# Where GpSimd's branch to the second path stands: behind the closing barrier, or in its own stream

## The chip, the cores and the metric

The kernel runs on one core of one Trainium2 chip. A core has five engines, each with an instruction stream of its own: TensorE (PE in the profile; its weight loads are shown apart as PEld), VectorE (DVE), ScalarE (ACT), GpSimd (POOL) and SyncE (SP). [...] The metric is the device time of one execution in microseconds (us), as the median of several runs. The profile's span is a shorter thing: it runs from the first to the last instruction of the program itself, and leaves out what the runtime does ahead of it and behind it.

## The reference: chunked attention, then a multiplicative feed-forward

```
# q, k, v: (8 batches, 8 heads, 576 rows, 64), in float32; chunks of 64 rows, so 9 a batch
scores = (1 / sqrt(64)) * q_chunk @ k_chunk.T     # 64 x 64, each chunk sees itself alone
scores = scores - max(scores, axis=-1)
attn   = exp(scores); attn = attn / (sum(attn, axis=-1) + 1e-9)
x      = (attn @ v_chunk), heads side by side     # 4608 tokens x 512
out    = ((x @ w1) * (x @ w2)) @ w3 @ w_out       # 512 -> 1024 -> 1024 -> 512, out 4608 x 512
```

## The kernel before

The program has two paths, and `tile_chunk_attention__then__multiplicative_ffn_kernel` (L536) joins them.

**The first path** (`fast_path`, L47) computes everything in bfloat16 on all engines. The 4608 tokens are cut into 18 steps of 256 (four chunks, `NP`), taken in pairs. Its work is written as short functions named by a letter, and the string `ORDER` (L9) lists by hand in which order they are called; every instruction keeps that order on its engine (`inorder`, L90). For step `p`: GpSimd issues the loads of q, k and v (L98), VectorE transposes q and k (`T`, L201), TensorE makes the scores (`S`), ScalarE takes their exponential (`E`, L234), TensorE multiplies by v, to which a column of ones is added so that the row sums come out beside the products (`P`). VectorE takes the reciprocal of the row sums into `rcs` (`N`, L261) and multiplies by it (L264). `X` and `H` put x into the layout that TensorE wants, `A` and `B` multiply by w1 and w2, `C` and `M` (L351, L366) form their product, `O` multiplies by `w3o`, which is w3 times w_out, made once on the chip (`V`, `W`, `Z`). `Y` (L396) copies the result out of PSUM and SyncE stores it (`Q`, L193). The last step, `O17` (L384 to L390), is copied and stored in three pieces.

**The check.** The first path takes no maximum off the scores, so it holds only while the row sums stay in a safe range. When the last reciprocals are there (L265), `do_check` (L270) counts in how many places `rcs` lies between 2^-60 and 2^60: two instructions on VectorE (L280, L281), then on GpSimd a sum over the partitions (L283), the number of places minus that sum as an integer, `bad` (L284), and a load of `bad` into a GpSimd register (L285). `ORDER` has nothing more for GpSimd after this. TensorE, VectorE, ScalarE and SyncE still have the last steps of the feed-forward ahead of them, down to `O17`.

**The closing.** L538 and L539 close the first path before the second one is written. The profile puts the closing's instructions under L539: SyncE waits for every semaphore of the first path, the last output stores among them; all engines meet at a barrier; GpSimd clears the semaphores; all engines meet again.

**The second path** (`second_path`, L452) does the whole computation again, slowly and with the maximum taken off, in float32 on GpSimd alone, and overwrites `out`. It stands under `with g.If(bad != 0)` (L501): GpSimd compares the register and, when `bad` is zero, jumps over the body. The body is long. The search for the row maximum alone (L516, L517) is written out 63 times, each with its wait and its clearing of the semaphore (`done`, L480), and no other engine has an instruction in it. With the inputs of this case `bad` is zero: the trace has no instruction of the body, and the branch at L501 is the last instruction of the span.

Of the kernel before, what the change touches and what calls it, by code (L numbers as in the profile page):

```python
# [43 lines left out]


@with_exitstack
def fast_path(  # L47
    ctx: ExitStack,
    tc: tile.TileContext,
    q: bass.AP,  # L50
# [8 lines left out]
    nc = tc.nc  # L59
    B, H, S, D = q.shape  # L60
# [3 lines left out]
    CH = 64  # L64
    NCH = S // CH
    NT = B * S
    DM = H * D
    DF = moe_w1.shape[1]
# [11 lines left out]
    f32 = mybir.dt.float32  # L80
# [23 lines left out]
    w1 = wpool.tile([P, KO, DF], bf, name="w1")  # L104
    w2 = wpool.tile([P, KO, DF], bf, name="w2")

    w3 = wpool.tile([P, DF // BL, DF // NB], bf, name="w3")
# [341 lines left out]
    return flag[0]  # L449


def second_path(tc, bad, q, k, v, w1, w2, w3, w_out, out):  # L452


    nc = tc.nc
    B, H, S, D = q.shape
    CH = 64
    NCH = S // CH
    DM, DF = w1.shape
    KB = 4  # L460
    f32 = mybir.dt.float32
    op = mybir.AluOpType
    g = nc.gpsimd
    with ExitStack() as ctx:
        def sb(name, *shape):
            return ctx.enter_context(nc.sbuf_tensor(name, [CH, *shape], f32))

        loaded = ctx.enter_context(nc.semaphore("loaded"))
        worked = ctx.enter_context(nc.semaphore("worked"))
        qt, kv, prod, s = sb("qt2", D), sb("kv2", CH, D), sb("prod2", CH, D), sb("s2", CH)  # L470
        m, e, euler, minus1 = sb("m2", 1), sb("e2", CH), sb("euler", CH), sb("minus1", 1)
        x, wb, a, b, o = sb("x2", DM), sb("wb2", KB, DF), sb("a2", DF), sb("b2", DF), sb("o2", DM)

        def move(dst, src):
            g.dma_start(dst, src).then_inc(loaded, 16)
            g.wait_ge(loaded, 16)
            g.dma_reset(range(loaded.num, loaded.num + 1))
            g.sem_clear(loaded)

        def done(ins):  # L480
            ins.then_inc(worked, 1)
            g.wait_ge(worked, 1)
            g.sem_clear(worked)

        def fold(t, n):
            while n > 1:
                n //= 2
                done(g.tensor_tensor(t(0, n), t(0, n), t(n, 2 * n), op.add))

        def times(dst, src, w, n, width):  # L490

            done(g.memset(dst[:], 0.0))
            p = prod[:].rearrange("c a b -> c (a b)")[:, 0:KB * width].rearrange("c (i n) -> c i n", i=KB)
            wt = wb[:, :, 0:width]
            with g.Fori(0, n // KB) as i:
                move(wt, w[bass.ds(i * KB, KB), :].partition_broadcast(CH))
                done(g.tensor_tensor(p, wt, src[:, bass.ds(i * KB, KB)].to_broadcast([CH, KB, width]), op.mult))
                fold(lambda lo, hi: p[:, lo:hi], KB)
                done(g.tensor_tensor(dst[:], dst[:], p[:, 0], op.add))

        with g.If(bad != 0):  # L501
            done(g.memset(euler[:], math.e))
            done(g.memset(minus1[:], -1.0))
            with g.Fori(0, B) as bi, g.Fori(0, NCH) as ci:
                with g.Fori(0, H) as hi:
                    def rows(t):
                        return t[bass.ds(bi, 1), bass.ds(hi, 1), bass.ds(ci * CH, CH), :]

                    move(qt[:], rows(q).rearrange("b h p d -> p (b h d)"))
                    move(kv[:], rows(k).rearrange("b h p d -> (b h p) d").partition_broadcast(CH))  # L510
                    done(g.tensor_tensor(prod[:], kv[:], qt[:].unsqueeze(1).to_broadcast([CH, CH, D]), op.mult))
                    fold(lambda lo, up: prod[:, :, lo:up], D)
                    done(g.tensor_scalar(s[:], prod[:, :, 0], 1.0 / math.sqrt(D), None, op.mult))
                    move(kv[:], rows(v).rearrange("b h p d -> (b h p) d").partition_broadcast(CH))
                    done(g.tensor_copy(m[:], s[:, 0:1]))
                    for j in range(1, CH):  # L516
                        done(g.tensor_scalar(m[:], m[:], s[:, j:j + 1], None, op.max))  # L517
                    done(g.tensor_scalar(s[:], s[:], m[:], -100.0, op.subtract, op.max))
                    done(g.tensor_tensor(e[:], euler[:], s[:], op.pow))
                    done(g.tensor_copy(s[:], e[:]))  # L520
                    fold(lambda lo, up: s[:, lo:up], CH)
                    done(g.tensor_scalar(m[:], s[:, 0:1], 1e-9, None, op.add))
                    done(g.tensor_tensor(m[:], m[:], minus1[:], op.pow))
                    done(g.tensor_scalar(e[:], e[:], m[:], None, op.mult))
                    done(g.tensor_tensor(prod[:], kv[:], e[:].unsqueeze(2).to_broadcast([CH, CH, D]), op.mult))
                    fold(lambda lo, up: prod[:, lo:up, :], CH)
                    done(g.tensor_copy(x[:, bass.ds(hi * D, D)], prod[:, 0, :]))
                times(a, x, w1, DM, DF)
                times(b, x, w2, DM, DF)
                done(g.tensor_tensor(b[:], a[:], b[:], op.mult))  # L530
                times(a, b, w3, DF, DF)
                times(o, a, w_out, DF, DM)
                move(out[bass.ds((bi * NCH + ci) * CH, CH), :], o[:])


def kernel(tc, *args):  # L536
    bad = fast_path(tc, *args)
    tc.close()  # L538
    tc.compile()  # L539
    second_path(tc, bad, *args)  # L540


# [28 lines left out]
```

## Time and profile before

| what | us |
|---|---|
| median of 3 runs | 247.47 (247.06 to 248.05) |
| the profiled execution's own time | 247.53 |
| its span, first to last instruction of the program | 243.1 |
| time of that execution outside its span | 4.43 |
| TensorE busy with matmuls | 225.4 (93% of the span) |
| VectorE, ScalarE, GpSimd busy | 154.4, 85.1, 83.7 |
| SyncE's last store issued (start) | 240.4 |

A line of the page or of an answer reads: line of the kernel, engine, operation, tile written <- tiles read, count, then durations. A `q` behind an engine's name means its sequencer: such instructions (waits, branches, register loads, barriers) are not counted as busy, and the timeline doesn't list them; the view of one source line does. There the three figures with slashes are the least, the middle and the greatest duration in ns, and the two behind them are the starts of the first and the last of them in us from the span's start.

### The profile page before, as it was taken

How to read it: one execution, taken by the hardware profiler on the slowest of the kernel's cores; microseconds unless marked ns; L12 is line 12 of the kernel's file. 1: busy time of each engine (PE TensorE's matmuls, PEld its weight loads, DVE VectorE, ACT ScalarE, POOL GpSimd, SP SyncE). 2: the span in 40 equal slices, each digit the busy share in tenths (PEclk: the TensorE clock that was granted, in tenths of full speed). 3: DMA queues.
4: the chain of work that ended last, by engine and by line, in shares of the span. 5: the costliest groups of instructions: out<-in, count | busy, mean ns of one | idle time of the engine just before them, and what ended most of it. 6: DMA issues, size and time to landing. Idle time of an engine off the chain costs nothing.

```text
span 243.1 us, 6361 instructions
## 1 busy us (share of the span) xinstructions
PE 225.4 (93%) x2731; PEld 120.0 (49%) x2753; DVE 154.4 (63%) x235; ACT 85.1 (35%) x116; POOL 83.7 (34%) x114
## 2 busy tenths in 40 slices
PE   1289999999999989999999999999999999999994
PEld 1147877874455444444444444444444444444443
DVE  1755899689799588999998899918540332143000
ACT  2411423423243343525336334162332332322322
POOL 7856874665995345574260230000000000000000
PEclk9999999999999999999999999999999999999999
DMA  6999999999999999999999893735502200400244
GB/s 174 179 185 181 185 169 199 197 191 172 166 171 219 213 234 241 176 219 200 207 222 241 230 150 84 168 88 206 143 0 89 86 0 0 175 1 1 86 173 173
DMA packets 93595, 37.63 MB, mean 155 GB/s; under 512 B 75008, under 2 KB 86528, under 8 KB 93568
## 3 DMA queue, kind: packets, MB, share of 16 engines
q0 software_dynamic: 82592, 18.88, 84.5%
q1 hardware_dynamic: 9936, 17.83, 24.5%
q10 hardware_dynamic: 1040, 0.52, 0.8%
q8 instruction: 21, 0.34, 0.6%
q14 instruction: 6, 0.05, 0.1%
HBM read 38.80 MB, written 9.44 MB: 198 GB/s over the span
## 4 chain that ended last, share of the span: by engine, by line
PE 89%; DMA 3%; DVE 3%; issue 2%; ACT 1%; SPq 1%; DVEq 0%
PE ab_ps L95 49%; PE o_ps L95 26%; PE w_ps L95 6%; PE pv L95 3%; PE s_ps L95 3%; PE z_ps L95 3%; DMA raw<-in_q_dram 2%; DVE qkT L201 1%; DMA qkm<-qkT 1%; SPq L193 1%; DVE xt L297 1%; DVE xn L264 1%; ACT qk L144 0%; ACT e L234 0%; DVE ab L366 0%
## 5 line engine op out<-in xcount | busy, mean ns | idle before, releaser
L95 PE MATMUL ab_ps<-xt,w 128*128 128x512 bf16 (+1 forms) x681 | 127.0, 342 | 0.9 <-DVE xt L297 0.3
L95 PEld LDWEIGHTS <-w 128*128 128x128 bf16 x704 | 67.1, 98 | 56.0 <-issue 1.8
L366 DVE TENSOR_TENSOR ab<-a_sb,ab_ps 128x512 bf16<-128x512 f32 x71 | 47.8, 674 | 43.6 <-ACT a_sb L351 43.4
L351 ACT COPY a_sb<-ab_ps 128x512 f32<-128x512 f32 x71 | 41.6, 586 | 80.8 <-PE ab_ps L95 80.6
L95 PE MATMUL o_ps<-w3o,ab 128*128 128x512 bf16 (+1 forms) x285 | 63.3, 373 | 0.6
L201 DVE STREAM_TRANSPOSE qkT<-qk 128x1024 bf16<-128x1024 bf16 x36 | 45.0, 1289 | 6.8 <-ACT qk L144 5.4
L95 PEld LDWEIGHTS <-ab 128*128 128x128 bf16 x296 | 28.5, 98 | 32.3
L98 POOL DMA_DIRECT2D vbuf<-in_v_dram x40 | 34.0, 856 | 19.8 <-PE ab_ps L95 4.9
L396 ACT COPY o_sb<-o_ps 128x1024 f32<-128x1024 f32 x17 | 17.2, 1013 | 45.3 <-PE o_ps L95 41.3
L264 DVE TENSOR_TENSOR xn<-pv,rcs 128x512 bf16<-128x512 f32 x36 | 24.9, 692 | 1.4
L98 POOL DMA_DIRECT2D qk<-in_q_dram x23 | 18.1, 791 | 9.8 <-DMA vbuf<-in_v_dram 2.5
L98 POOL DMA_DIRECT2D qk<-in_k_dram x23 | 18.0, 782 | 6.8 <-DMA vbuf<-in_v_dram 4.5
L234 ACT ACTIVATE e<-s_ps 128x1024 bf16<-128x1024 f32 x16 | 15.9, 1028 | 2.2 <-PE s_ps L95 2.0
L95 PE MATMUL w_ps<-wo,w3T 128*128 128x512 bf16 x62 | 13.9, 379 | 0.1
L305 DVE STREAM_TRANSPOSE xm<-xn 128x512 bf16<-128x512 bf16 x20 | 13.5, 696 | 0.2
L261 DVE RECIPROCAL rcs<-pv 128x8 f32<-128x8 f32 x36 | 7.0, 193 | 10.4 <-PE pv L95 10.4
L98 POOL DMA_DIRECT2D w<-in_moe_w_dram x16 | 11.1, 695 | 5.4 <-DMA vbuf<-in_v_dram 1.8
L95 PEld LDWEIGHTS <-e 64*32 64x32 bf16 (+1 forms) x832 | 7.8, 97 | 8.6 <-issue 6.8
L95 PE MATMUL pv<-vbuf,e 64*32 64x65 bf16 (+1 forms) x832 | 10.2, 198 | 1.6 <-ACT e L234 1.1
L297 DVE STREAM_TRANSPOSE xt<-xn 128x512 bf16<-128x512 bf16 x16 | 11.4, 711 | 0.5
L95 PEld LDWEIGHTS <-qkT 32*64 32x64 bf16 x512 | 5.6, 117 | 10.6 <-DVE qkT L201 7.9
L389 DVE COPY o_sb<-o_ps 128x256 f32<-128x256 f32 x1 | 0.4, 425 | 16.0 <-PE o_ps L95 16.0
(29 smaller groups left out, 53.7 us busy)
## 6 DMA issues: line engine op xcount, KB each, us to landing
out_dram<-o_sb SPq DMA_DIRECT2D x17, 512.0 KB, 2.9
qkm<-qkT SPq DMA_DIRECT2D x40, 128.0 KB, 4.4
vbuf<-in_v_dram POOLq DMA_DIRECT2D x32, 128.0 KB, 8.1
w<-in_moe_w_dram POOLq DMA_DIRECT2D x16, 256.0 KB, 9.6
qk<-in_q_dram POOLq DMA_DIRECT2D x11, 256.0 KB, 7.4
qk<-in_k_dram POOLq DMA_DIRECT2D x11, 256.0 KB, 7.8
xt<-xm SPq DMA_DIRECT2D x40, 64.0 KB, 3.1
wo<-in_moe_w_out_dram POOLq DMA_DIRECT2D x4, 256.0 KB, 7.9
```

Source lines behind the costliest of these rows:

```text
L95: return inorder(nc.tensor.matmul(*a, **kw))
L98: return inorder(nc.gpsimd.dma_start(dst, src))
L193: inorder(nc.sync.dma_start(dst, src))
L201: inorder(nc.vector.transpose(qkT_t[g][:, :, p % 2, s, heads(h)].rearrange("p e h (y t) -> p h t e y", t=2), qk_t[p][:, s, heads(h)].rearr ...
L234: inorder(nc.scalar.activation(e_t[p][:, :, heads(hh)], s_t[p][:].rearrange("p u (h q) -> p u h q", q=CH)[:, :, heads(hh)], Exp, scale=sca ...
L261: inorder(nc.vector.reciprocal(rc, pv[:, :, :, D:W]))
L264: inorder(nc.vector.tensor_mul(xn_t[p][:, u], pv[:, :, :, 0:D], rc.to_broadcast([P, 2, 4, D])))
L297: inorder(nc.vector.transpose(new_xt(g)[:].rearrange("p (o t) -> p o t", o=KO)[:, :, t0:t0 + UT] .rearrange("p o (m y) -> p m o y", y=BL), ...
L305: inorder(nc.vector.transpose(xm_t[g][:, u, :, m].rearrange("p o (c y) -> p c o y", y=BL), xn_t[p][:].rearrange("p u r m d -> p (u r) m d" ...
L351: inorder(nc.scalar.copy(a_t[p, j][:], ps_t[p, j][:, 0, :]))
L366: inorder(nc.vector.tensor_mul(o, view(a_t.pop((p, j))[:]), view(ps_t.pop((p, j))[:, 1, :])))
L396: inorder(nc.scalar.copy(o_sb[:], ps_t.pop(p)[:]))
```

## The change

The branch and the body of the second path move into the same tile program as the first path. `second_path` is called while that program is still open; `g.If` becomes `tc.If`, and the body becomes a critical section that GpSimd itself guards (`sync_engine` Pool, without a drain of GpSimd). The body's buffers come from a tile pool in place of raw tensors, and its two semaphores from the program's own allocator. The two lines that closed the first path ahead of the second one are gone: the program closes once, when the caller's `with` ends (L566 of before). The operations of the body are the same, one level less indented. `fast_path` is renamed `first_path` and is otherwise as it was.

```diff
-def fast_path(
+def first_path(
...
-def second_path(tc, bad, q, k, v, w1, w2, w3, w_out, out):
+@with_exitstack
+def second_path(ctx, tc, bad, q, k, v, w1, w2, w3, w_out, out):
...
-    with ExitStack() as ctx:
+    pool = ctx.enter_context(tc.tile_pool(name="second", bufs=1))
+    with tc.If(bad != 0), tc.tile_critical(sync_engine=mybir.EngineType.Pool, no_gpsimd_drain=True):
         def sb(name, *shape):
-            return ctx.enter_context(nc.sbuf_tensor(name, [CH, *shape], f32))
-
-        loaded = ctx.enter_context(nc.semaphore("loaded"))
-        worked = ctx.enter_context(nc.semaphore("worked"))
+            return pool.tile([CH, *shape], f32, name=name)
+
+        loaded, worked = tc.alloc_semaphore("loaded"), tc.alloc_semaphore("worked")
...
-        with g.If(bad != 0):
-            done(g.memset(euler[:], math.e))
-            done(g.memset(minus1[:], -1.0))
...
+        done(g.memset(euler[:], math.e))
+        done(g.memset(minus1[:], -1.0))
...
 def tile_chunk_attention__then__multiplicative_ffn_kernel(tc, *args):
-    bad = fast_path(tc, *args)
-    tc.close()
-    tc.compile()
-    second_path(tc, bad, *args)
+    second_path(tc, first_path(tc, *args), *args)
```

More of the change, by code (lines that the diff above doesn't have):

```diff
@@ L499, in times @@
                 done(g.tensor_tensor(dst[:], dst[:], p[:, 0], op.add))
-        with g.If(bad != 0):
-            done(g.memset(euler[:], math.e))
-            done(g.memset(minus1[:], -1.0))
[L504 to L533, printed above, removed]
@@ new lines, in second_path, with rows @@
+        done(g.memset(euler[:], math.e))
+        done(g.memset(minus1[:], -1.0))
+        with g.Fori(0, B) as bi, g.Fori(0, NCH) as ci:
+            with g.Fori(0, H) as hi:
+                def rows(t):
+                    return t[bass.ds(bi, 1), bass.ds(hi, 1), bass.ds(ci * CH, CH), :]
+                move(qt[:], rows(q).rearrange("b h p d -> p (b h d)"))
+                move(kv[:], rows(k).rearrange("b h p d -> (b h p) d").partition_broadcast(CH))
+                done(g.tensor_tensor(prod[:], kv[:], qt[:].unsqueeze(1).to_broadcast([CH, CH, D]), op.mult))
+                fold(lambda lo, up: prod[:, :, lo:up], D)
+                done(g.tensor_scalar(s[:], prod[:, :, 0], 1.0 / math.sqrt(D), None, op.mult))
+                move(kv[:], rows(v).rearrange("b h p d -> (b h p) d").partition_broadcast(CH))
+                done(g.tensor_copy(m[:], s[:, 0:1]))
+                for j in range(1, CH):
+                    done(g.tensor_scalar(m[:], m[:], s[:, j:j + 1], None, op.max))
+                done(g.tensor_scalar(s[:], s[:], m[:], -100.0, op.subtract, op.max))
+                done(g.tensor_tensor(e[:], euler[:], s[:], op.pow))
+                done(g.tensor_copy(s[:], e[:]))
+                fold(lambda lo, up: s[:, lo:up], CH)
+                done(g.tensor_scalar(m[:], s[:, 0:1], 1e-9, None, op.add))
+                done(g.tensor_tensor(m[:], m[:], minus1[:], op.pow))
+                done(g.tensor_scalar(e[:], e[:], m[:], None, op.mult))
+                done(g.tensor_tensor(prod[:], kv[:], e[:].unsqueeze(2).to_broadcast([CH, CH, D]), op.mult))
+                fold(lambda lo, up: prod[:, lo:up, :], CH)
+                done(g.tensor_copy(x[:, bass.ds(hi * D, D)], prod[:, 0, :]))
+            times(a, x, w1, DM, DF)
+            times(b, x, w2, DM, DF)
+            done(g.tensor_tensor(b[:], a[:], b[:], op.mult))
+            times(a, b, w3, DF, DF)
+            times(o, a, w_out, DF, DM)
+            move(out[bass.ds((bi * NCH + ci) * CH, CH), :], o[:])
```

## The prediction

> **What bounds the kernel now.** I read the page first, for the engine that fills the span.
>
> ```profile
> span 243.1 us, 6361 instructions
> ...
> PE 225.4 (93%) x2731; PEld 120.0 (49%) x2753; DVE 154.4 (63%) x235; ACT 85.1 (35%) x116; POOL 83.7 (34%) x114
> ...
> POOL 7856874665995345574260230000000000000000
> ...
> PE 89%; DMA 3%; DVE 3%; issue 2%; ACT 1%; SPq 1%; DVEq 0%
> ```
>
> TensorE makes 89% of the chain that ended last. GpSimd's row of slices (6.08 us each) goes empty in its last third. Nothing that GpSimd does there is on the chain within the span. So a change to GpSimd alone can win only at the very end, where all engines must meet, and I looked there next: GpSimd's timeline from 135 us on, then the source lines that the change touches.
>
> ```profile
> 140.28 1.79 POOL L98 DMA_DIRECT2D vbuf<-in_v_dram  x2
> 169.47 0.35 POOL L283 CROSS_LANE_REDUCE all_good<-good 128x1 f32<-128x1 f32 x1 [27.41 <-DVE both L281]
> 169.92 0.18 POOL L284 TENSOR_SCALAR bad<-all_good 1x1 int32<-1x1 f32 x1
> ```
>
> ```profile
> L285 POOLq TENSOR_LOAD <-bad x1: 746/746/746, 170.1 to 170.1; - x1
> ```
>
> ```profile
> L539 SPq EVENT_SEMAPHORE  x12: 17/28/28, 240.7 to 243.0; - x12
> L539 POOLq EVENT_SEMAPHORE  x4: 17/17/17, 242.3 to 243.0; - x4
> L539 POOLq DRAIN  x3: 46/92/971, 171.0 to 242.8; - x3
> ```
>
> ```profile
> L501 POOLq COMPARE_BRANCH  x1: 50/50/50, 243.1 to 243.1; - x1
> ```
>
> `bad` is in GpSimd's register at 170.1 + 0.75 = 170.9 us. GpSimd then begins the closing's drain (171.0) and does nothing until the closing barrier (242.3 to 243.0). Only behind that barrier comes the branch, as the last instruction of the span. Its 50 ns look like nothing. But 247.53 - 243.1 = 4.43 us of this execution lie outside the span, and the branch stands at their head. The DMA view of the stretch 243.1 to 248 us (40 slices of 0.12 us) shows what happened in them:
>
> ```profile
> GB/s 0 0 0 0 0 0 0 0 0 0 67 0 0 0 0 0 0 0 0 0 0 0 0 0 0 0 0 67 0 0 0 0 0 0 0 0 0 0 0 0
> DMA packets 2, 0.02 MB, mean 3 GB/s; under 512 B 0, under 2 KB 0, under 8 KB 0
> ## 3 DMA queue, kind: packets, MB, share of 16 engines
> q14 instruction: 2, 0.02, 1.0%
> ```
>
> Two packets of instructions, and nothing else. By the trace's own records they are 8192 bytes each; the first starts at 244.334 and takes 0.307. The trace also keeps every update of every semaphore, past the last instruction too. Semaphore 2, which no instruction of the program uses, counts the engines in before the runtime resets the others: 243.333, 243.367, then nothing until 246.464, then 246.507, 246.530 and on. In the next round of the same semaphore the steps are 247.538, .572, .610, .654, .677, so 34, 38, 44 and 23 ns. **The third arrival is late.** It should come 38 ns after the second, at 243.405, and comes 3.059 us later; the fourth follows it by the usual 43 ns, so nobody else was late by then. All other engines left the closing barrier at the same 243.05; only GpSimd had something between, the branch. I read this as GpSimd jumping to a place whose instructions weren't in its buffer, fetching them (the packet begins 1.2 us after the branch), and the whole core waiting for it.
>
> **The change part by part.**
>
> *The branch moved to the register load.* Its cost where it stands now: 246.464 - 243.405 = 3.06 us, all on the path that sets the end. Where it will stand: about 170.9 us, plus 0.05 for itself, plus the same 3.06, so GpSimd is through by some 174.1 us (177.5 if a second fetch is paid as well). Its next appointment is the closing barrier at 242.3 us: 65 us of cover or more, TensorE's matmuls of steps 14 to 17 being what hides it. If the cover were gone, the price would be the 3.06 again. It issues no DMAs of data; its instruction fetch, 8 KB a packet, meets SyncE's last transposing moves (L193, the last at 174.4) for some 0.3 us on one queue, and none of those is near the chain. GpSimd's own queue is empty by then: its last load is at 140.28.
>
> *What the 3.06 us leave late next.* Without the branch, GpSimd leaves its last barrier instruction at 243.0 + 0.02, ahead of the others (243.04 to 243.05), and the first engine reached semaphore 2 at 243.333, 0.3 us after that. If GpSimd needs no longer, it is third at 243.405 as the chain wants. No row shows GpSimd's own way from there without a miss, so I bound it. At best it is on time and the gain is 3.06. At worst all that lies between the packet's landing (244.641) and its arrival (246.464), 1.82 us, is its own work rather than the fetch; then it arrives at 243.01 + 1.82 = 244.84 and the gain is 246.46 - 244.84 = 1.62. I take 3.06, because in the next round of that barrier GpSimd's place in the chain costs 38 ns, no more than the others', and because this is the nearest row.
>
> *The closing itself* stays one closing: the same waits of SyncE, two barriers and a clear. The section may add a semaphore or two to SyncE's waits. They go by at about 61 ns each (240.73 to 242.25), and only those behind the last store's landing (242.06) count: 0 to 0.12 us. It may as easily reorder them in our favour by as much. I take 0.
>
> *Buffers and semaphores.* The body's pool lies over memory that the first path has used, and the body writes `out`, so the section must wait for nearly everything. Inside the jumped-over body these waits cost nothing. Ahead of the branch they would cost the gain (first rival below).
>
> Sum: 247.53 - 3.06 + 0 = 244.47 against the profiled execution; that stands 0.06 above the median of the runs, so I forecast **244.4**, 1.2% less. Its own range is 243.9 to 245.0, from the 1 us that the runs before spread over.
>
> [...] The row has 50 ns for the instruction but 3.06 us until the engine is seen again. [...]
>
> **The rivals.**
>
> *Part of the gap is GpSimd's own* (above): 247.47 - 1.62 = 245.9. For it: 1.8 us pass after the packet has landed, and I don't see what fills them. Against: the 38 ns.
>
> *The change doesn't do what it says:* the waits for memory and `out` are put ahead of the branch. Then GpSimd branches when the last store has landed, 242.06 + 0.05, is back after 3.06 at 245.2, the closing barrier (242.34 to 243.08, 0.74 us) follows to 245.9, and 0.33 later the chain's third arrival is at 246.25, against 246.46 before. That is 247.47 - 0.2 = 247.3, no change. For it: the section does depend on all of that. Against: the section stands inside the If, and its waits with it.
>
> *Slower:* the region is fenced, all engines meeting before the branch and again behind it, since a region that is scheduled as one piece may be closed off so. The If comes last in the program, so both fences stand at the end, at the price of the closing's own row, 0.74 us each, with the branch and its fetch still between: 247.47 + 1.47 = 248.9 (a single fence gives 248.2, within 0.5%). It decides as soon as an engine other than GpSimd has an instruction of the If. Against: only GpSimd holds the register and works in the body.
>
> **How the numbers follow.** Chances: forecast 0.70, part of the gap 0.13, waits ahead of the branch 0.12 (a single fence is counted here), two fences 0.05. 0.5% is 1.24 us, about what a measurement of this kernel can tell from no change. Faster by more is the first two, 0.83; same is 0.12; slower 0.05. The range takes in the first two with their spread: 243.9 to 246.1.
>
> **What would show it.** Right: the span still near 242.8 to 243.1, now ending with the closing's semaphores and not with a branch; the COMPARE_BRANCH at 171 to 172 us; an instruction packet about 1.2 us behind it; no packet right behind the span's end; semaphore 2 counting through without a gap, and time outside the span down from 4.43 to about 1.4 us. The second rival would show the branch still at 242 us; the third, barrier rows of the If on several engines; the first, a gap of some 1.5 us left before the third arrival with no branch in front. The prediction is wrong above all if GpSimd, having jumped early, must fetch again at the end: its closing and the runtime's part lie right behind the target and should come in sequence, but no row shows that.

## The result, and the profile after

The changed kernel takes 244.23 us (median of 4 runs, 243.97 to 245.27) against 247.50 (247.06 to 248.05, now four runs, the profiled one counted): a ratio of 0.9875 with a 95% interval of 0.9839 to 0.9911. The profiled execution took 244.48 us, with a span of 242.9.

The lines of the page that answer to those of before:

```profile
span 242.9 us, 6385 instructions
...
PE 226.7 (93%) x2753; PEld 120.2 (49%) x2753; DVE 154.3 (64%) x235; ACT 85.2 (35%) x116; POOL 83.7 (34%) x114
...
POOL 7856976656986345764160230000000000000000
...
PE 72%; DMA 16%; DVE 4%; SPq 3%; POOL 2%; issue 1%; ACT 0%; DVEq 0%; POOLq 0%
```

Within the span nothing has moved: the engines' busy times and GpSimd's empty last third are those of before. (TensorE's 226.7 us against 225.4 go with 22 more matmul records; a second execution of the changed kernel, e10 below, has 225.6 with the count of before.) TensorE's share of the chain fell from 89% to 72%, but that isn't the change: between loads and transposes that end nearly together the chain is followed back by one or the other, and a second execution of the same changed kernel shows 70%.

The branch and the closing, by source line:

```profile
L466 POOLq EVENT_SEMAPHORE  x2: 17/17/17, 173.6 to 173.7; - x2
L466 POOLq COMPARE_BRANCH  x1: 45/45/45, 170.8 to 170.8; - x1
```

```profile
L563 SPq EVENT_SEMAPHORE  x12: 17/28/28, 240.6 to 242.9; - x12
L563 POOLq EVENT_SEMAPHORE  x4: 17/17/17, 242.2 to 242.8; - x4
L563 POOLq DRAIN  x3: 46/98/971, 173.8 to 242.7; - x3
```

The branch itself still takes 45 ns, and GpSimd's next instruction starts 2.75 us after it (170.828 to 173.579). The two fetches that used to stand behind the span have come along. The first (171.81 to 172.42) lies between the branch and that next instruction; the second starts at 174.20, when GpSimd has already gone on. The DMA view of 170.8 to 175 us has both among SyncE's moves:

```profile
q1 hardware_dynamic: 324, 0.43, 40.8%
q14 instruction: 2, 0.02, 1.6%
```

and the same view of 242.9 to 248 us is empty:

```profile
GB/s 0 0 0 0 0 0 0 0 0 0 0 0 0 0 0 0 0 0 0 0 0 0 0 0 0 0 0 0 0 0 0 0 0 0 0 0 0 0 0 0
DMA packets 0, 0.00 MB, mean 0 GB/s; under 512 B 0, under 2 KB 0, under 8 KB 0
```

Semaphore 2 now counts 243.162, 243.197, 243.411, 243.455, 243.478, and its last update is at 244.843 instead of 247.895. From GpSimd's last closing semaphore (242.995 before, 242.824 after) to that last update it is **4.90 us before and 2.02 after: 2.88 us less**. The other 0.17 of the 3.05 by which the two profiled executions differ is an earlier arrival at the closing: TensorE's last matmul ends at 239.64 in place of 239.81. Spans of one kernel scatter by more than that (242.4 to 243.7 over the four runs of after), so I don't put it down to the change.

### The profile page after: what moved, and what is told of

It reads as the page before. It is cut to its first block, busy times and chain, and to the rows that moved or that the text cites. A ratio compares the mean times of both kernels' runs of the same rounds, so it can differ in the third digit from the quotient of the medians.

```text
span 242.9 us, 6385 instructions
## 1 busy us (share of the span) xinstructions
PE 226.7 (93%) x2753; PEld 120.2 (49%) x2753; DVE 154.3 (64%) x235; ACT 85.2 (35%) x116; POOL 83.7 (34%) x114
## 4 chain that ended last, share of the span: by engine, by line
PE 72%; DMA 16%; DVE 4%; SPq 3%; POOL 2%; issue 1%; ACT 0%; DVEq 0%; POOLq 0%
PE ab_ps L95 39%; PE o_ps L95 23%; PE w_ps L95 6%; DMA w<-in_moe_w_dram 4%; DMA qkm<-qkT 3%; SPq L193 3%; DMA qk<-in_q_dram 3%; DMA qk<-in_k_dram 3%; DMA xt<-xm 3%; PE pv L95 2%; PE s_ps L95 2%; DVE qkT L201 2%; POOL vbuf L98 1%; POOL w L98 1%; DVE xt L297 1%
```

## The experiments

My theory: a jump whose target is far ahead in GpSimd's stream makes it fetch instructions, and whoever waits for GpSimd waits for that. The first rival: it is the place that costs, a second piece of program behind the closing, whatever the jump's length. The second: the early section gains or costs something by its form. Medians scatter by some 0.5 us here, so beside them I use the **tail**, a number that doesn't depend on the matmuls: from the start of GpSimd's last closing semaphore to the runtime's last update of semaphore 2, by the trace's records.

| kernel | median us | ratio to before (95% interval) | tail us | third arrival after the second, us |
|---|---|---|---|---|
| before | 247.50 | | 4.90 | 3.097 |
| after | 244.23 | 0.9875 (0.9839 to 0.9911) | 2.02 | 0.214 |
| e1 short body, late branch | 245.12 | 0.9918 (0.9901 to 0.9934) | 2.35 | 0.392 |
| e2 short body, early branch | 245.10 | 0.9907 (0.9889 to 0.9924) | 2.02 | 0.214 |
| e3 no second path | 244.78 | 0.9895 (0.9878 to 0.9911) | 2.01 | 0.202 |
| e4 two late branches | 250.47 | 1.0138 (1.0121 to 1.0155) | 7.77 | 5.934 |
| e5 jump over some 214 | 247.42 | 1.0001 (0.9985 to 1.0017) | 4.81 | 2.975 |
| e6 jump over some 118 | 245.08 | 0.9917 (0.9894 to 0.9939) | 2.83 | 0.751 |
| e7 early branch, late count | 248.44 | 1.0062 (1.0038 to 1.0086) | 2.02 | 0.214 |
| e8 as e2, padded | 244.52 | 0.9884 (0.9865 to 0.9904) | 2.01 | 0.202 |
| e9 as e1, padded | 245.26 | 0.9915 (0.9894 to 0.9936) | 2.20 | 0.392 |
| e10 after, again | 244.70 | 0.9882 (0.9860 to 0.9905) | 2.04 | 0.214 |
| e11 no second path, again | 244.29 | 0.9884 (0.9856 to 0.9911) | 2.03 | 0.201 |

e5 was run eight times, e6 twice, after and the other experiments four times each. Each ratio is to runs of before on the same chip: 247.22 for e1 to e4, 247.08 for e5 to e7, 247.44 for e8 to e11.

**e1: the late branch with a short body.**

```diff
         with g.If(bad != 0):
             done(g.memset(euler[:], math.e))
             done(g.memset(minus1[:], -1.0))
-            with g.Fori(0, B) as bi, g.Fori(0, NCH) as ci:
-                with g.Fori(0, H) as hi:
...
-                move(out[bass.ds((bi * NCH + ci) * CH, CH), :], o[:])
```

> The kernel before, with the branch still behind the closing barrier, but the body of the second path cut to its first two fills (its loops are left out; they don't run on these inputs), so that the jump lands a few instructions on. Theory (the price is the fetch of a far target): no instruction packet behind the span, semaphore 2 counts through, and the time falls by what the change saved, to 244.3 (244.0 to 244.7), with the branch still the span's last instruction. Rival (the price is that a branch, or a second piece of program, stands behind the closing at all): 247.5 as before.

The branch is still the last instruction of the span, and nothing is fetched behind it (source line, then DMA view of 242.9 to 248 us):

```profile
L501 POOLq COMPARE_BRANCH  x1: 50/50/50, 242.9 to 242.9; - x1
```

```profile
DMA packets 0, 0.00 MB, mean 0 GB/s; under 512 B 0, under 2 KB 0, under 8 KB 0
```

The time falls by 2.10 us and the tail by 2.55. The rival, "the place costs", would have left 247.5 and is out: the length of the jump is what costs. I had expected 244.0 to 244.7 and got 245.12; 0.33 of the tail stays, which e9 takes apart.

**e2: the early branch with the same short body.** The same loops are left out of the changed kernel.

> The changed kernel with the same cut body (loops left out). Theory: GpSimd goes on within 0.2 us of the branch at 170.8, not 2.75 us; the time doesn't move, 244.2 (243.9 to 244.6), since 65 us covered the fetch. Rival (the early branch still cost something at the end, by its section's semaphores and boundary): below 243.7.

GpSimd goes on 0.19 us after the branch, and the tail is the changed kernel's to a hundredth:

```profile
L466 POOLq EVENT_SEMAPHORE  x2: 17/17/17, 171.5 to 171.6; - x2
L466 POOLq COMPARE_BRANCH  x1: 45/45/45, 171.3 to 171.3; - x1
```

So the 2.75 us that follow the branch in after, at 171 us, are covered wholly (tail 2.02 in both). The median of 245.10 is above what I expected. Part of it is in the closing of the profiled execution, which lies ahead of the tail: 1.01 us between GpSimd's two releases of the barrier, where after has 0.57 (see e8).

**e3 and e11: no second path.** The two closing lines and the call of `second_path` are taken out of before.

```diff
     bad = fast_path(tc, *args)
-    tc.close()
-    tc.compile()
-    second_path(tc, bad, *args)
```

> The kernel before without any second path (the whole of it left out), the count and the load of bad kept. Theory: 244.2 (243.9 to 244.6), as after: nothing of the branch is left on the path. In the changed kernel the third arrival at semaphore 2 comes 0.214 us after the second instead of 0.038; if that is GpSimd's own work behind the last barrier it shows here too, if it belongs to the section it is gone and the time is 0.18 lower. Rival (the section costs time elsewhere): 243.5 or less.

> The kernel without any second path once more, beside the changed one. Theory (the changed kernel has nothing of the branch left on its path): the same time within 0.4 us. Rival (the early section costs something yet): faster than the changed kernel by 0.5 us or more.

The tail is 2.01 and 2.03 us. The third arrival comes 0.20 us after the second here too, without any branch: that is GpSimd's own. In both traces L285 has only a wait of 17 ns, so the load of `bad`, which was to be kept, is out as well; it stood in GpSimd's idle stretch.

> The changed kernel, unaltered, on the chip of the runs beside it, to be set against the one without a second path. 2.01 us from GpSimd's last closing semaphore to the runtime's last count, a time of 244.3 (243.9 to 244.9).

The changed kernel took 244.70 us here, with a tail of 2.04. The medians miss two of the expectations narrowly: e3's 244.78 is above 244.6, and e11's 244.29 is 0.41 below e10, where 0.4 was named. The single runs of each spread over 0.7 to 1.1 us, and the ratios, 0.9882 and 0.9884, are alike. Nothing of the branch is left that these runs could tell, and no run points to a version that beats the changed kernel.

**e4: two far jumps in a row.** `second_path` is called twice behind the closing, with buffers and semaphores of their own.

> The kernel before with the second path written twice, one behind the other, each with its own branch behind the closing barrier: two far jumps in a row. Theory (each far jump is a fetch): one more packet pair and one more stall of 2.75 to 3.1 us, 250.2 to 250.6. Rival (a price paid once, for leaving the first program late): 247.6.

250.47 us, 3.25 above before, and the tail 2.87 longer. The two branches and their packets (source line, then DMA view of 243 to 251 us, 0.2 us a slice):

```profile
L501 POOLq COMPARE_BRANCH  x2: 50/50/50, 243.0 to 245.6; - x2
```

```profile
GB/s 0 0 0 0 41 0 0 0 0 0 0 0 0 0 0 0 41 0 41 0 0 0 0 0 0 0 0 0 0 0 0 0 41 0 0 0 0 0 0 0
DMA packets 4, 0.03 MB, mean 4 GB/s; under 512 B 0, under 2 KB 0, under 8 KB 0
```

Each jump pays; a price paid once would have left 247.6. From one branch to the next it is 2.61 us.

**e5 and e6: how far is far.** The feed-forward part of the second path's body is left out of before (e5), and in e6 its search for the maximum is cut to 16 columns too (`range(1, CH // 4)`).

> The kernel before with the feed-forward part of the second path's body left out: the jump at the end goes over some 214 instructions instead of some 300. Theory (the target must lie beyond what GpSimd holds): still beyond, 247.5, with packets behind the span. If what is held reaches further than I think, 244.3.

> As the run before it, and the search for the maximum cut to 16 of 64 columns (that part of the second path is left out too): the jump goes over some 118 instructions. [...]

Over some 214 instructions all but 0.1 us of the price is paid (tail 4.81), with two packets behind the span (DMA view of e5, 242.9 to 248 us):

```profile
q14 instruction: 2, 0.02, 1.2%
```

Over some 118 it is only 0.8 us more than with no branch (tail 2.83), with one packet in place of two (DMA view of e6, 242.8 to 248 us, 0.13 us a slice):

```profile
GB/s 0 0 0 0 0 0 0 0 63 0 0 0 0 0 0 0 0 0 0 0 0 0 0 0 0 0 0 0 0 0 0 0 0 0 0 0 0 0 0 0
...
q14 instruction: 1, 0.01, 0.6%
```

For a branch at this place, then, nearly the full price begins somewhere between the two. Neither of the two times that I had named for e6, 244.3 and 247.5, came; it is 245.08. The packet starts at 243.88, 0.09 us after the third arrival, so that arrival doesn't wait for it. It is still 0.54 us later than after's, and the runtime's resets take another 0.27 (1.06 us between the two rounds of semaphore 2, where after has 0.79). Of the 0.54, 0.18 is what a late branch costs in e1 too. The 0.36 left is near the pause of 0.31 that e2 and e8 show below; whether it is the same thing, these runs don't tell.

**e7: the early branch with no cover.** The count is taken out of the last `N` and called behind the last step of `ORDER`.

```diff
-        if p == NP - 1 and u == 1:
-            do_check()
...
         do[step[0]](*(int(n) for n in step[1:].split(".") if n))
+    do_check()
     return flag[0]
```

> The changed kernel with the count of good rows moved behind the last step (after the last copy of o_sb on VectorE), so that the branch in GpSimd's own stream has no cover left. Worked out from the changed kernel's rows: VectorE's last copy ends at 240.16, the count takes 0.89 to GpSimd's sum, 1.49 from there to the branch (242.5), 2.75 for the fetch (245.3), then the drain of 0.97 and the closing barrier of 0.67 instead of the stores' wait: 248.5 (247.3 if the drain is short), slower than before the change. Rival (the gain came from the section's form, not from its cover): 245 to 246, the count's own 1.5 to 2 us alone.

248.44 us, slower than before the change. The branch and the closing's drain (two source lines):

```profile
L465 POOLq EVENT_SEMAPHORE  x2: 17/17/17, 244.9 to 245.0; - x2
L465 POOLq COMPARE_BRANCH  x1: 45/45/45, 242.1 to 242.1; - x1
```

```profile
L562 SPq EVENT_SEMAPHORE  x12: 17/28/3998, 240.5 to 246.8; - x12
L562 POOLq DRAIN  x3: 46/98/971, 245.1 to 246.6; - x3
```

From the branch to GpSimd's next instruction it is 2.79 us (242.083 to 244.870), GpSimd's drain of 0.97 follows, and one of SyncE's waits is 4.0 us long, until GpSimd's two semaphores at L465 are through. The form of the section is the changed kernel's, the tail too (2.02); only the cover is gone. GpSimd's first release of the closing comes 3.90 us later than in after (246.07 against 242.17). Of that, 2.60 is the far jump beyond e2's near one; the rest is the late count and the drain. So it is the idle time of GpSimd that makes the change a gain, not the section's form.

**e8 and e9: where a block of instructions ends.** In these traces GpSimd's instructions come in packets of 8192 bytes. I call what one packet holds a block, and going on from one block to the next in sequence a crossing. Fills of one element on GpSimd are put ahead of L285, twelve in e2's kernel and 48 in e1's, to shift where the blocks end. (In e9's trace nearly all the fills run behind the load of `bad`; they are ahead of the closing all the same.)

```diff
+        for _ in range(12):
+            inorder(nc.gpsimd.memset(tick[:], 0.0))
         flag.append(nc.gpsimd.value_load(bad[:]))
```

> The changed kernel with the cut body, and twelve fills of one element on GpSimd ahead of the load of bad, where GpSimd has 65 us to spare. Without them GpSimd paused 0.39 us between its second closing semaphore and the drain behind it, with an instruction packet 0.69 us after that drain began. Theory (the stream crosses into a new block of instructions there, and a crossing costs some 0.3 to 0.4 us when others wait): twelve more instructions put the crossing ahead of the closing barrier, the pause is 0.08, the closing takes 0.67 instead of 1.1, no packet after 242 us. Rival (a chance delay of that execution): the pause stays, or appears elsewhere.

> The kernel before with the cut body, branch behind the closing barrier, and 48 such fills. Without them, 2.35 us passed from GpSimd's last closing semaphore to the runtime's last count, against 2.01 with no branch there and 4.90 with the far one. Theory (of the 0.33 some 0.18 are the branch itself and 0.15 a crossing of blocks in what the runtime does behind it): with the crossing moved ahead of the closing 2.19 remain. Rival (a branch at the end costs 0.33 wherever the blocks lie): 2.35.

In e2 the drain in the middle of the closing took 232 ns and came 0.39 us after the semaphore ahead of it, where after has 98 ns and 0.08; a packet of instructions follows at 243.9 us (source line, then the DMA view of 242 to 249 us; the slices are 0.175 us, the small entry at the left is the end of a store):

```profile
L533 POOLq DRAIN  x3: 46/232/971, 171.7 to 243.7; - x3
```

```profile
GB/s 24 0 0 0 0 0 0 0 0 0 47 0 0 0 0 0 0 0 0 0 0 0 0 0 0 0 0 0 0 0 0 0 0 0 0 0 0 0 0 0
...
q14 instruction: 1, 0.01, 0.4%
```

That packet starts only after the drain is over (243.44), so the drain didn't wait for it. What the pause itself is, the runs don't show; but it comes and goes with the packet. Twelve instructions more, and that packet is at 172.8 us, in the idle stretch; GpSimd's two releases of the closing are 0.57 us apart instead of 1.01, and the drain is back at 103 ns. The pause has moved along: from the branch to GpSimd's next instruction it is now 0.50 us, where e2 has 0.19 (two source lines of e8):

```profile
L535 POOLq DRAIN  x3: 46/103/971, 172.3 to 242.3; - x3
```

```profile
L468 POOLq EVENT_SEMAPHORE  x2: 17/17/17, 172.1 to 172.2; - x2
L468 POOLq COMPARE_BRANCH  x1: 54/54/54, 171.6 to 171.6; - x1
```

In e9 the runtime's resets, 0.94 us between its two rounds in e1, are back at 0.79, and the tail is 2.20 us, as worked out: a late branch to a near target costs 0.19, and 0.15 goes when the blocks are shifted. That this 0.15 was a crossing in what the runtime does is my reading; e1 has no packet there that would show it. Both forecasts on crossings held. In e8 the median falls with the closing, from 245.10 to 244.52, though the intervals of the two ratios overlap; the tail, which begins behind the closing, stays (2.02 and 2.01). In e9 the median doesn't fall: 0.15 is less than the scatter.

## Why the prediction was right

**The place of the loss.** That the whole core waits for GpSimd behind the span, because of its jump, is shown by e1 (a near target: 2.55 us off the tail), e4 (a second jump: 2.87 on it) and e3 (none: 2.01 left). That the target's instructions were missing from a buffer is my reading of the packets, two behind the far jump and none behind e1's; how much GpSimd holds, no run shows.

**The size.** The prediction had 3.06 us on the path; the tails give 2.88. The step that was mis-sized is the third arrival: I took it to come 38 ns after the second, as in the other round. It comes 0.20 to 0.21 us after it in after and in every run without a late branch, also in the kernel without a second path. So 0.18 of the gap was GpSimd's own. The first rival (1.62 of gain left, 1.82 its own) had the right idea at ten times the size. The profiled time came out at 244.48 against 244.47 only because that execution reached its closing 0.17 us sooner; that is luck. The 3.27 between the medians contains scatter of the same kind: e10 and its runs of before are 2.74 apart, and the 2.88 of the tails lies between.

**The cover.** The jump costs 2.75 us at 171 us, not 3.06, with GpSimd due at 242.2. e2 and e10 show that nothing of it reaches the end (tails of 2.02 and 2.04 against 2.01 and 2.03 without a second path), e7 what comes when it is not covered (248.44).

**The closing** cost what it did: 0.57 us between GpSimd's two releases, before and after. That GpSimd would have to fetch again at the end, the sign named as the worst, didn't come in after; in e2 the two releases are 1.01 us apart, with an instruction packet at 243.9 us, behind the pause. That this 0.44 more is a price of that kind is not shown.

**The second and third rival** fell with the trace: the branch is at 170.8 us, so no wait stands ahead of it, and no other engine has an instruction of L466. The second rival's sum left out GpSimd's drain, which in e7 takes its 0.97 us behind the branch: by the same sum with it, an estimate, waits ahead of the branch would have given 248.3 and not 247.3.

**What would show it** came as named: the span at 242.9 without a branch at its end, the packets behind the early branch (the first 0.93 us behind its end, where I had said 1.2), none at the end; time outside the span 1.55 us where I had said 1.4, by the same mis-sized step.

**Three slips** in the working change nothing in the forecast. Two fetches would have been over at 177.1 us and not at 177.5. Ahead of TensorE at 171 us were also the products of steps 12 and 13 and the outputs from step 9 on, and not only steps 14 to 17. And the rival that the paragraph on buffers calls the first is the second.

**The branch and the packets by themselves.** To a near target it is 0.19 us from the branch to GpSimd's next instruction in e2, of which some 0.08 is what other neighbouring closing instructions of GpSimd take too, so some 0.11 are left; to the far one it is 2.75 in after and 2.79 in e7. In e9 a packet didn't stop GpSimd: the fills around the one at 174.3 us go on at an even 0.15 us.

**Still open:** what fills the time after the packet's landing. In after the first packet lands at 172.42 and GpSimd goes on 1.16 us later, before the second packet starts. What the pause of e2 and e8 is. And why e6's jump over some 118 instructions still costs 0.8 us.

## What to carry to other kernels

Look behind the span: here 4.43 us lay outside it with two instruction packets among them, while GpSimd, which had jumped last, held the whole core; after the change it was 1.55 us and no packet. The branch over code that rarely runs was worth putting as early as its condition is known, on an engine with idle time left: its price lay in how far it jumped (2.75 us over the whole body, 0.19 over two fills) and not in the branch (45 ns); without that idle time the same move lost (e7, 248.44 us). If it can't go early, keep the body short: here a late jump over a few instructions cost 0.19 us once the blocks were shifted, one over some 118 cost 0.8, and one over some 214 nearly all of the 2.88.

## What the runs showed of the hardware that was not expected

Twelve idle instructions ahead took 0.44 us from between the two barriers of a closing (e2 1.01, e8 0.57), and with them an instruction packet went from 243.9 to 172.8 us; 48 took 0.15 from the runtime's resets (e1 0.94, e9 0.79). That both were crossings from one block of instructions to the next is my reading. And GpSimd, as I read the third arrival, is late at the runtime's first round even with nothing in front of it: 0.20 us after the second in e3 and e11.
